# Row sums moved to ScalarE for half of an attention kernel, and mask additions to VectorE for the other half

## The chip, the core and the metric

The kernel runs on one core of one Trainium2 chip. A core has five engines that run their own instruction queues side by side: TensorE (PE, with its weight loads shown apart as PEld), VectorE (DVE), ScalarE (ACT), GpSimd (POOL) and SyncE (SP), which here only starts transfers. The metric is device time in microseconds (us) of one execution; lower is better.

## The reference, cut to what matters

Attention over a window of 64 positions, then a gated feed-forward layer, then a layer of 8 experts of which each token uses one. Only the attention is touched.

```python
batch, n_heads, seq, head_dim = (4, 8, 576, 64)

def _attn_ref(q, k, v):
    scale = 1.0 / np.sqrt(D)
    scores = scale * np.matmul(q, k.transpose(0, 1, 3, 2))
    rel = pos[:, None] - pos[None, :]
    mask = (rel >= 0) & (rel < 64)
    scores = np.where(mask, scores, -1000000000.0)
    scores = scores - np.max(scores, axis=-1, keepdims=True)
    attn = np.exp(scores)
    attn = attn / (np.sum(attn, axis=-1, keepdims=True) + 1e-09)
    return np.matmul(attn, v)

# x = attention output as 2304 x 512
h = (x @ w1) * (x @ w2) @ w3 @ w_out     # first layer, d_ff 1024
# second layer: e = argmax(h @ w_gate); out = gate * relu(h @ w1[e]) @ w2[e]
```

## The kernel before, in words

**Attention.** The 4 batches of 8 heads are handled as 16 pairs of heads, n = 0 to 15, four pairs to a batch (NP is 4). A pair is cut into three groups g, each of three tiles of 128 x 128 scores, so there are 48 groups. A group goes through these steps:

- `score` (L141, L145), PE: a matmul of the identity `idb` with a bf16 mask writes 0 or -1e30 into a PSUM buffer `sps` of 384 columns, and three fp32 matmuls of k and q add the scores to it. Each fp32 matmul shows as two PE instructions.
- `top` (L151, L154), DVE: the maximum of each row, and its negative times 0.125.
- `exps` (L163), ACT: three exponentials of 128 x 128, from `sps` into `pp`.
- `recip` (L168, L170, L172), DVE: the row sums of `pp`, plus 1e-9, and their reciprocal `r`. The small results stand in spare columns of `sps`, so this step ends the use of that buffer.
- `normal` (L177), POOL: `pp` times `r`.
- `turn` (L184), PE: three transposes into a buffer `tps` of the same tag "S", of which there are two in all. `keep` (L189), ACT, copies it out.
- `pv` (L201), PE, and `x_high`, `x_low` (L213, L217) on ACT and DVE make the tokens of the next layer.

**The weights.** The first layer's weights arrive as 64-bit words in 40 chunks. Three DVE instructions for each chunk (L506, L508, L513) turn them into fp32, then ACT (L527) and POOL (L531) split them into a high and a low part. W3 and W_out are multiplied on PE beforehand (L540). The second input matrix can be converted only when all of that product is done, because it takes the slots of W_out.

**The first layer.** For each of nine units of 256 tokens and each of eight steps: two blocks of 12 matmuls (L560), a product and a split on DVE and ACT (L565, L568, L572, L576), and a block of six matmuls (L584). The experts' layer follows.

**Order.** A planner (`Plan`) takes each step with its engine, an assumed duration, a rank and the buffers that it takes and gives, and puts the steps into one order by a simulated list schedule. The order in which instructions are issued on every engine is fixed by that when the program is built, and each engine then takes its instructions strictly in that order. A changed duration of a step can thus move any other step.

Of the kernel before, what the change touches and what calls it, by code (L numbers as in the profile page):

```python
# [9 lines left out]
F32 = mybir.dt.float32  # L10
# [4 lines left out]
AF = mybir.ActivationFunctionType  # L15
ALU = mybir.AluOpType
AX = mybir.AxisListType.X
# [3 lines left out]
B, H, S, D = 4, 8, 576, 64  # L21
NT, DM, DF, NE = B * S, H * D, 1024, 8
NP = H // 2
# [9 lines left out]
class Plan:  # L33
# [5 lines left out]
    def __init__(self, bufs):  # L39
        self.bufs, self.t, self.tag = bufs, [], {}  # L40
# [74 lines left out]
class Attention:  # L115
# [5 lines left out]


    GW = 384

    def __init__(self, tc, pool, ps_s, ps_v, ps_ab, qkv, xunit, ident):
        self.tc, self.nc, self.pool, self.ps_s, self.ps_v = tc, tc.nc, pool, ps_s, ps_v
# [10 lines left out]
    def score(self, n, g):  # L137

        nc, s = self.nc, self.s[n]
        ps = s["S", g] = self.ps_s.tile([128, 512], F32, name="sps", tag="S")  # L140
        nc.tensor.matmul(ps[:, 0:self.GW], lhsT=self.idb, rhs=self.mask[1 if g else 0].rearrange("p a b -> p (a b)"),  # L141
                         start=True, stop=False)
        for i in range(3):
            c = 3 * g + i
            nc.tensor.matmul(ps[:, 128 * i:128 * i + 128], lhsT=s["q"][:, 128 * c:128 * c + 128],  # L145
                             rhs=s["k"][:, 64 * c:64 * c + 128], start=False, stop=i == 2)

    def top(self, n, g):
        nc, s = self.nc, self.s[n]
        ps = s["S", g]  # L150
        nc.vector.tensor_reduce(out=ps[:, 384:387], in_=ps[:, 0:self.GW].rearrange("p (a b) -> p a b", a=3),  # L151
                                axis=AX, op=ALU.max)
        nm = s["nm", g] = self.pool.tile([128, 3], F32, name="nm", tag="nm", bufs=4)
        nc.vector.tensor_scalar(nm, ps[:, 384:387], -0.125, None, op0=ALU.mult)  # L154

    def exps(self, n, g):
        nc, s = self.nc, self.s[n]
        ps = s["S", g]
        nm = s.pop(("nm", g))
        p = s["p", g] = self.pool.tile([128, self.GW], F32, name="pp", tag="pp", bufs=3)  # L160
        for i in range(3):
            o = slice(128 * i, 128 * i + 128)
            nc.scalar.activation(out=p[:, o], in_=ps[:, o], func=AF.Exp, bias=nm[:, i:i + 1], scale=0.125)  # L163

    def recip(self, n, g):
        nc, s = self.nc, self.s[n]
        ps = s.pop(("S", g))
        nc.vector.tensor_reduce(out=ps[:, 392:395], in_=s["p", g].rearrange("p (a b) -> p a b", a=3),  # L168
                                axis=AX, op=ALU.add)
        nc.vector.tensor_scalar(ps[:, 400:403], ps[:, 392:395], 1e-9, None, op0=ALU.add)  # L170
        r = s["r", g] = self.pool.tile([128, 3], F32, name="r", tag="r", bufs=4)
        nc.vector.reciprocal(out=r, in_=ps[:, 400:403])  # L172

# [12 lines left out]
    def keep(self, n, g):  # L186
        s = self.s[n]
        PT = s["PT", g] = self.pool.tile([128, self.GW], F32, name="PT", tag=f"PT{g}", bufs=1)
        self.nc.scalar.activation(out=PT, in_=s.pop(("tp", g))[:, 0:self.GW], func=AF.Copy)  # L189

# [28 lines left out]
    def plan(self, P, n, r, done):  # L219


        def add(name, eng, us, dr, fn, after=(), *a, **kw):
            done[name, n] = P.add(eng, us, r + dr, lambda: fn(n, *a), [done[x] for x in after if x in done], **kw)

        def N(*names):
            return [(x, n) for x in names]

        for i, x in enumerate("qkv"):
            add(x, "DMA", (1.5, 0.8, 1.5)[i], -18 + i, self.load, (), i, take=[(x, (x, n))], lat=2.0)
        for g in range(3):  # L230
            q = -12 + 2 * g
            add(("sc", g), "PE", 0.55, q, self.score, N("q", "k"), g, take=[("S", ("S", n, g))],
                give=[("q", n), ("k", n)] if g == 2 else [])
            add(("top", g), "DVE", 0.72, q, self.top, N(("sc", g)), g)
            add(("exp", g), "ACT", 1.02, q, self.exps, N(("top", g)), g, take=[("pp", ("pp", n, g))])
            add(("rec", g), "DVE", 0.9, q, self.recip, N(("exp", g)), g, give=[("S", n, g)])
            add(("nor", g), "POOL", 0.85, q, self.normal, N(("rec", g)), g)
            add(("tu", g), "PE", 0.36, q, self.turn, N(("nor", g)), g, take=[("S", ("TP", n, g)), (f"PT{g}", ("PT", n, g))],
                give=[("pp", n, g)])
            add(("kp", g), "ACT", 0.5, q, self.keep, N(("tu", g)), g,  # L240
                give=[("TP", n, g)])
        add("pv", "PE", 1.4, -2, self.pv, N("v", *[("kp", g) for g in range(3)]),
            take=[("pv", ("pv", n)), ("ab", ("pvt", n))], give=[("v", n)] + [("PT", n, g) for g in range(3)])
        for tail in (1, 0):
            pc = pieces(n, tail)
            for i, (t0, t1, u, c0) in enumerate(pc):
                us = 0.15 + 0.001 * (t1 - t0)
                give = [("pvt" if tail else "pv", n)] if i == len(pc) - 1 else []
                add(("xh", tail, i), "ACT", us, -1, self.x_high, N("pv") + [("free", u)], tail, i)
                add(("xl", tail, i), "DVE", us, -1, self.x_low, N(("xh", tail, i)), tail, i, give=give)  # L250
                done.setdefault(("unit", u), []).append(done[("xl", tail, i), n])
        done["x", n] = done[("xl", tail, i), n]
# [20 lines left out]
def pieces(n, tail):  # L273

    b = n // NP
    t, end = (512, S) if tail else (0, 512)
    out = []
    while t < end:
        u, c0 = divmod(S * b + t, UNIT)
        w = min(UNIT - c0, end - t)  # L280
        out.append((t, t + w, u, c0))
        t += w
    return out
# [113 lines left out]
def attention_moe_moe_kernel(ctx: ExitStack, tc: tile.TileContext, q0, k0, v, w1, w2, w3, w_out,  # L397
# [316 lines left out]
    def early_rows(part):  # L714

        if part == 0:
            rt.count(256)
            t = idx["early"] = exp_state["p"].tile([128, 2, 2], I32, name="ixe", tag="ixe")
            nc.sync.dma_start(out=t, in_=tab[0:256, :].rearrange("(j p) x -> p j x", p=128))
            g = xg["early"] = moe.tile([128, 4, DM], F32, name="xt1", tag="xt1")  # L720
            nc.vector.memset(g[:, 0:2, :], 0.0)
        else:
            j = part - 1
            top = UNIT * (NU - 1)
            nc.gpsimd.indirect_dma_start(out=xg["early"][:, j, :], out_offset=None, in_=x2d[0:top, :],
                                         in_offset=bass.IndirectOffsetOnAxis(ap=idx["early"][:, j, 0:1], axis=0),
                                         bounds_check=top - 1, oob_is_err=False)
# [375 lines left out]
```

## Time and profile before

| | us |
|---|---|
| median of 3 runs | 787.07 |
| lowest and highest | 786.39, 788.73 |
| the profiled execution | 785.67 |
| its span (first to last instruction) | 784.0 |
| PE busy, share of the span | 734.4, 94% |
| DVE busy | 377.2, 48% |
| ACT busy | 302.0, 39% |

The profile is that of one execution of 785.67 us, of which 1.67 lie outside the span. The shares of the whole span say little here, since the stages differ: in the first 125 us the weights are converted and the first five or so head pairs are done, up to about 440 us the first layer and the rest of the attention run, and the experts fill the rest. The rows below are therefore taken by stage.

### The profile page before, as it was taken

What the parts mean: (1) busy time and instruction counts of PE and PEld (TensorE: products, weight loads), DVE (VectorE), ACT (ScalarE), POOL (GpSimd) and SP (SyncE); (2) the same over time, 40 slices, a digit from 0 to 9 for tenths busy, and PEclk for the clock granted to TensorE, in tenths of its full rate; (3) what the DMA queues carried; (4) which work ended last, traced back from release to release, by engine and by line L of the source; (5) the groups of instructions that cost most, each with busy time, mean ns of one, the idle gap of its engine ahead of it and who ended that gap; (6) DMA issues with size and microseconds to landing.
All of it is one profiled execution on the core that took longest, in us unless ns stands there. A gap on an engine that the chain in (4) does not pass through costs nothing. (4 is left out here: it accounts for less than half of the span.)

```text
span 784.0 us, 13573 instructions
## 1 busy us (share of the span) xinstructions
PE 734.4 (94%) x5227; PEld 658.0 (84%) x5227; DVE 377.2 (48%) x907; ACT 302.0 (39%) x683; POOL 168.1 (21%) x196
## 2 busy tenths in 40 slices
PE   3799989999999999999999999879999999999995
PEld 2577778999999999999999998767888998988874
DVE  6987995543544444444324233813534661661110
ACT  2554443433333243344222123524445563553221
POOL 6554553110111311110020001123112212111010
PEclk9999998999999999999999999999999999999998
DMA  8946762421322222005000001783726772750010
GB/s 326 408 167 217 213 210 84 152 79 31 111 91 87 78 77 77 31 28 189 28 1 28 1 28 48 244 174 109 247 88 233 258 246 90 251 156 28 5 41 14
DMA packets 38934, 97.47 MB, mean 124 GB/s; under 512 B 9748, under 2 KB 9876, under 8 KB 38849
## 3 DMA queue, kind: packets, MB, share of 16 engines
q1 hardware_dynamic: 33072, 83.06, 32.0%
q0 software_dynamic: 4816, 12.77, 5.0%
q8 instruction: 50, 0.82, 0.5%
q10 hardware_dynamic: 960, 0.53, 0.2%
q14 instruction: 36, 0.29, 0.1%
HBM read 86.83 MB, written 10.65 MB: 124 GB/s over the span
## 5 line engine op out<-in xcount | busy, mean ns | idle before, releaser
L560 PE MATMUL ab<-xt,w 128*128 128x256 f32 x1728 | 229.2, 287 | 0.1
L560 PEld LDWEIGHTS ab<-xt,w 128*128 128x128 f32 x1728 | 219.1, 193 | 4.8 <-DVE f L513 0.3
L584 PE MATMUL acc<-w,gt 128*128 128x512 f32 x432 | 114.4, 399 | 3.4 <-ACT gt L572 2.6
L584 PEld LDWEIGHTS acc<-w,gt 128*128 128x128 f32 x432 | 76.1, 189 | 17.4 <-ACT gt L572 3.1
L568 DVE TENSOR_TENSOR a_sb<-ab,a_sb 128x256 f32<-128x256 f32 x72 | 30.5, 423 | 121.9 <-PE ab L560 113.5
L908 PE MATMUL yps<-w,hT 128*128 128x512 f32 x336 | 82.3, 395 | 0.0
L177 POOL TENSOR_TENSOR pp<-pp,r 128x384 f32<-128x384 f32 x48 | 39.6, 828 | 191.7 <-DVE r L172 160.5
L908 PEld LDWEIGHTS yps<-w,hT 128*128 128x128 f32 x336 | 61.3, 188 | 11.6
L572 ACT ACTIVATE gt<-a_sb 128x256 fp32r<-128x256 f32 x72 | 30.0, 416 | 100.3 <-DVE a_sb L568 95.6
L684 DVE TENSOR_TENSOR w<-ck,w 128x1024 fp32r<-128x1024 f32 x48 | 58.1, 1220 | 21.0 <-ACT w L680 14.4
L540 PE MATMUL wps<-w,w3T 128*128 128x512 f32 x192 | 52.7, 417 | 11.7 <-ACT w3T L527 11.6
L680 ACT ACTIVATE w<-ck 128x1024 fp32r<-128x1024 f32 x48 | 50.3, 1057 | 27.0 <-DMA ck<-in_moe_w 24.4
L900 POOL DMA_INDIRECT out<-y,idx x20 | 20.1, 1003 | 178.5 <-ACT y L899 124.1
L163 ACT ACTIVATE pp<-sps,nm 128x128 f32<-128x128 f32 x144 | 42.3, 368 | 39.4 <-DVE nm L154 37.2
L540 PEld LDWEIGHTS wps<-w,w3T 128*128 128x128 f32 x192 | 35.5, 196 | 19.4 <-ACT w3T L527 11.6
L927 PEld LDWEIGHTS hps<-exT,w 128*128 128x128 f32 x384 | 46.4, 192 | 3.5 <-issue 2.2
L927 PE MATMUL hps<-exT,w 128*128 128x256 f32 x384 | 47.4, 284 | 1.9 <-PEq L1049 0.9
L565 ACT ACTIVATE a_sb<-ab 128x256 f32<-128x256 f32 x72 | 27.8, 386 | 55.1 <-PE ab L560 51.9
L389 POOL DMA_INDIRECT tab<-ent,pos x18 | 17.6, 980 | 139.5 <-DVE pos L376 42.2
L422 DVE TENSOR_TENSOR exT<-gps,exT 128x512 fp32r<-128x512 f32 x23 | 15.9, 691 | 58.9 <-ACT exT L421 58.9
L576 DVE TENSOR_TENSOR gt<-a_sb,gt 128x256 fp32r<-128x256 f32 x72 | 31.3, 434 | 25.4 <-ACT gt L572 24.4
L145 PE MATMUL sps<-k,q 128*128 128x128 f32 x288 | 41.4, 282 | 1.0 <-DMA k<-in_k 1.0
(132 smaller groups left out, 1025.6 us busy)
## 6 DMA issues: line engine op xcount, KB each, us to landing
ck<-in_moe_w SPq DMA_DIRECT2D x88, 512.0 KB
q<-in_q SPq DMA_DIRECT2D x16, 576.0 KB
v<-in_v SPq DMA_DIRECT2D x16, 576.0 KB
k<-in_k SPq DMA_DIRECT2D x16, 320.0 KB
w<-in_moe_w_out SPq DMA_DIRECT2D x8, 512.0 KB
w<-in_moe_w SPq DMA_DIRECT2D x8, 512.0 KB
x2d<-x SPq DMA_DIRECT2D x16, 256.0 KB
x2d<-x ACTq DMA_DIRECT2D x2, 256.0 KB
```

Of the source, the lines that this page charges most:

```text
L145: nc.tensor.matmul(ps[:, 128 * i:128 * i + 128], lhsT=s["q"][:, 128 * c:128 * c + 128], rhs=s["k"][:, 64 * c:64 * c + 128], start=False, s ...
L163: nc.scalar.activation(out=p[:, o], in_=ps[:, o], func=AF.Exp, bias=nm[:, i:i + 1], scale=0.125)
L177: nc.gpsimd.tensor_tensor(p, p, s.pop(("r", g)).unsqueeze(2).to_broadcast([128, 3, 128]), op=ALU.mult)
L540: mm(ps, lhsT=t[:, a, 128 * j:128 * j + 128], rhs=wo[b][:, o:o + 512], start=g == 0 and j == 0 and x == 0, stop=g == 1 and j == 3 and x == 2)
L560: mm(ps, lhsT=w[a][:, c:c + 128], rhs=x[:, b, kk, :], start=kk == 0 and i == 0, stop=kk == 3 and i == 2)
L568: V.tensor_tensor(asb[u, m], gps.pop((u, m, 1)), asb[u, m], op=ALU.mult)
L576: V.tensor_tensor(g[:, 1, :], asb.pop((u, m)), g[:, 0, :].bitcast(F32), op=ALU.subtract)
L584: mm(accs[u][t], lhsT=g[:, a, 128 * t:128 * t + 128], rhs=ws["w34"][b][:, 512 * m:512 * m + 512], start=m == 0 and i == 0, stop=m == 7 and ...
L680: nc.scalar.activation(out=eparts()[0], in_=eq[0], func=AF.Copy)
L684: low.tensor_tensor(lo, eq.popleft(), hi.bitcast(F32), op=ALU.subtract)
L908: mm(ps, lhsT=hT[f][:, a, c0:c0 + 128], rhs=w[b][:, 512 * f:512 * f + 512], start=f == 0 and i == 0, stop=f == 7 and i == 2)
L927: mm(ps[:, 0:256], lhsT=w1e[a][:, c:c + 128], rhs=xT[:, b, kk, :], start=kk == 0 and i == 0, stop=kk == 3 and i == 2)
```

## The change

The first two batches (n below `SUMS` = 8, 24 groups) no longer sum `pp` on DVE. The three exponentials of a group write their row sums themselves, through ACT's accumulator output, into a small tile `rs`, and `recip` starts from that. In the last two batches (n from `LATE` = 8 on, 24 groups) the mask matmul is gone from `score`; `top` adds the mask to the scores in PSUM on DVE before the maximum is taken. The planner's assumed durations of these steps are changed to match.

```diff
+    SUMS = 2 * NP
+    LATE = 2 * NP
 ... score
-        nc.tensor.matmul(ps[:, 0:self.GW], lhsT=self.idb, rhs=self.mask[1 if g else 0].rearrange("p a b -> p (a b)"),
-                         start=True, stop=False)
+        late = n >= self.LATE
+        if not late:
+            nc.tensor.matmul(ps[:, 0:self.GW], lhsT=self.idb,
+                             rhs=self.mask[1 if g else 0].rearrange("p a b -> p (a b)"), start=True, stop=False)
...
-                             rhs=s["k"][:, 64 * c:64 * c + 128], start=False, stop=i == 2)
+                             rhs=s["k"][:, 64 * c:64 * c + 128], start=late, stop=late or i == 2)
 ... top
+        if n >= self.LATE:
+            sc = ps[:, 0:self.GW].rearrange("p (a b) -> p a b", a=3)
+            nc.vector.tensor_tensor(sc, sc, self.mask[1 if g else 0], op=ALU.add)
 ... exps
+        rs = s["rs", g] = self.pool.tile([128, 3], F32, name="rs", tag="rs", bufs=4) if n < self.SUMS else None
-            nc.scalar.activation(out=p[:, o], in_=ps[:, o], func=AF.Exp, bias=nm[:, i:i + 1], scale=0.125)
+            nc.scalar.activation(out=p[:, o], in_=ps[:, o], func=AF.Exp, bias=nm[:, i:i + 1], scale=0.125,
+                                 **({} if rs is None else dict(accum_out=rs[:, i:i + 1])))
 ... recip
+        rs = s.pop(("rs", g))
+        if rs is None:
+            rs = ps[:, 392:395]
+            nc.vector.tensor_reduce(out=rs, in_=s["p", g].rearrange("p (a b) -> p a b", a=3), axis=AX, op=ALU.add)
+        nc.vector.tensor_scalar(ps[:, 400:403], rs, 1e-9, None, op0=ALU.add)
 ... plan (the assumed durations, us)
-            add(("top", g), "DVE", 0.72, q, self.top, N(("sc", g)), g)
+            add(("top", g), "DVE", 1.28 if late else 0.72, q, self.top, N(("sc", g)), g)
...
```

The other assumed durations go from 0.55 to 0.38 for the late `score`, from 1.02 to 1.65 for the early `exps` and from 0.9 to 0.4 for the early `recip`.

The first place is on DVE, late in the conversion of the weights, between the maximum of one group and the reciprocal of the same or a near one (`bits` and `f` are the conversions, `a_sb` and `gt` the first layer). Before:

```order
L151 TENSOR_REDUCE sps<-sps 128x3
L506 TENSOR_SCALAR bits<-ck 128x512 x2
L508 SCALAR_TENSOR_TENSOR bits<-ck,bits 128x512 x2
L513 SCALAR_TENSOR_TENSOR f<-ck,bits 128x512 x2
L568 TENSOR_TENSOR a_sb<-ab,a_sb 128x256
L168 TENSOR_REDUCE sps<-pp 128x3
L506 TENSOR_SCALAR bits<-ck 128x512
L170 TENSOR_SCALAR sps<-sps 128x3
L508 SCALAR_TENSOR_TENSOR bits<-ck,bits 128x512
L172 RECIPROCAL r<-sps 128x3
```

The corresponding place now:

```order
L158 TENSOR_REDUCE sps<-sps 128x3
L518 TENSOR_SCALAR bits<-ck 128x512
L161 TENSOR_SCALAR nm<-sps 128x3
L518 TENSOR_SCALAR bits<-ck 128x512
L520 SCALAR_TENSOR_TENSOR bits<-ck,bits 128x512 x2
L525 SCALAR_TENSOR_TENSOR f<-ck,bits 128x512 x2
L580 TENSOR_TENSOR a_sb<-ab,a_sb 128x256
L181 TENSOR_SCALAR sps<-rs 128x3
L158 TENSOR_REDUCE sps<-sps 128x3
L183 RECIPROCAL r<-sps 128x3
```

The sum has left the queue and its successor reads `rs`; six conversions still stand between the maximum and it. On PE, this stretch had two score steps, a block L584, a block L560 and another L584 ahead of the next transposes. Now two score steps, one block of six (L596) and three blocks of twelve (L572) stand there.

The second place is on PE at the first group of the third batch, where a block of the first layer ends. Before:

```order
L560 MATMUL ab<-xt_372,w_1108 128x256
L141 LDWEIGHTS idb
L141 MATMUL sps<-mask_113,idb 128x384
L145 MATMUL sps<-k,q 128x128 x3
L141 LDWEIGHTS idb
L141 MATMUL sps<-mask_114,idb 128x384
L145 MATMUL sps<-k,q 128x128 x3
```

The same place now:

```order
L572 MATMUL ab<-xt_378,w_1107 128x256 x2
L572 MATMUL ab<-xt_378,w_1108 128x256
L149 MATMUL sps<-k,q 128x128 x6
L572 MATMUL ab<-xt_132,w_948 128x256 x2
L572 MATMUL ab<-xt_132,w_949 128x256
```

A weight load and a matmul of 384 columns are gone from each group. Between the second and the third score step stood a block L560, a block L584, another L560 and one step of transposes; now two blocks L572 and one L596 stand there.

The third place is on DVE for the same groups. Before:

```order
L568 TENSOR_TENSOR a_sb<-ab,a_sb 128x256
L151 TENSOR_REDUCE sps<-sps 128x3
L576 TENSOR_TENSOR gt<-a_sb,gt 128x256
L154 TENSOR_SCALAR nm<-sps 128x3
L151 TENSOR_REDUCE sps<-sps 128x3
L154 TENSOR_SCALAR nm<-sps 128x3
L168 TENSOR_REDUCE sps<-pp 128x3
L170 TENSOR_SCALAR sps<-sps 128x3
L172 RECIPROCAL r<-sps 128x3
```

And now:

```order
L580 TENSOR_TENSOR a_sb<-ab,a_sb 128x256
L157 TENSOR_TENSOR sps<-sps,mask_113 128x384
L588 TENSOR_TENSOR gt<-a_sb,gt 128x256
L158 TENSOR_REDUCE sps<-sps 128x3
L157 TENSOR_TENSOR sps<-sps,mask_114 128x384
L161 TENSOR_SCALAR nm<-sps 128x3
L158 TENSOR_REDUCE sps<-sps 128x3
L161 TENSOR_SCALAR nm<-sps 128x3
L180 TENSOR_REDUCE sps<-pp 128x3
L580 TENSOR_TENSOR a_sb<-ab,a_sb 128x256
L181 TENSOR_SCALAR sps<-sps 128x3
L180 TENSOR_REDUCE sps<-pp 128x3
```

Each group has one more instruction, the addition L157, ahead of its maximum, and the second group's addition stands between the first group's maximum and its `nm`.

## Rows read from the trace of the kernel before

**Rows 1.** Stages: length, busy us (instructions) of PE, PEld, DVE, ACT, POOL, PEclk, DMA.

```profile
0.00:40.00 40.00, 22.23 (x129) 16.28 (x130) 32.65 (x76) 16.35 (x38) 24.46 (x53) 0.96 0.95 368
40.00:94.00 54.00, 50.56 (x344) 40.20 (x344) 45.59 (x103) 25.18 (x62) 26.36 (x24) 1.00 0.60 192
94.00:125.00 31.00, 25.64 (x170) 23.46 (x168) 28.12 (x61) 14.71 (x36) 18.76 (x17) 0.89 0.58 198
125.00:440.00 315.00, 314.96 (x2632) 294.78 (x2631) 133.91 (x424) 109.12 (x313) 40.99 (x47) 1.00 0.21 70
```

**Rows 2.** PE's waits from 0 to 125 us: us in total, times, longest.

```profile
PE wps L540 <- ACT w3T L527: 11.6, 1, 11.6
PE tps L184 <- DVE r L172: 7.4, 4, 3.5
PE tps L184 <- POOL pp L177: 2.4, 3, 1.6
...
PE sps L141 <- DVE r L172: 0.9, 1, 0.9
```

**Rows 3.** Timeline of PE, first groups of the third batch: start, duration, line.

```profile
206.67 0.34 PE L141 MATMUL sps<-mask,idb 128*128 128x384 bf16 x1
206.84 0.83 PE L145 MATMUL sps<-k,q 128*128 128x128 f32 x6
207.51 0.33 PE L141 MATMUL sps<-mask,idb 128*128 128x384 bf16 x1
207.67 0.83 PE L145 MATMUL sps<-k,q 128*128 128x128 f32 x6
208.26 1.67 PE L560 MATMUL ab<-xt,w 128*128 128x256 f32 x12
209.77 1.55 PE L584 MATMUL acc<-w,gt 128*128 128x512 f32 x6
211.16 1.59 PE L560 MATMUL ab<-xt,w 128*128 128x256 f32 x12
```

**Rows 4.** Line 141, the whole span: count, ns minimum, median and maximum.

```profile
L141 PEld LDWEIGHTS <-idb x48: 95/96/153, 13.5 to 347.6; 128*128 128x128 bf16 x48
```

**Rows 5.** Timeline of DVE: the reciprocal of the first of these groups.

```profile
210.57 0.18 DVE L172 RECIPROCAL r<-sps 128x3 f32<-128x3 f32 x1
```

**Rows 6.** Groups of DVE's additions and products from PSUM by shape.

```profile
L568 DVE TENSOR_TENSOR a_sb<-ab,a_sb 128x256 f32<-128x256 f32 x72 | 30.5, 423 | 121.9 <-PE ab L560 113.5 <-PE tps L184 3.5 <-issue 2.9
L548 DVE TENSOR_TENSOR w<-wps,w 128x512 fp32r<-128x512 f32 x8 | 5.4, 679 | 2.5 <-ACT w L544 2.5
```

**Rows 7.** Line 168 up to 119.8 us, and up to 94 us.

```profile
L168 DVE TENSOR_REDUCE sps<-pp x16: 544/552/561, 18.8 to 117.2; 128x3 f32<-128x384 f32 x16
...
L168 DVE TENSOR_REDUCE sps<-pp x13: 549/552/561, 18.8 to 87.4; 128x3 f32<-128x384 f32 x13
```

**Rows 8.** Timeline of PE, then of DVE, around PE's longest wait after its start.

```profile
119.30 0.87 PE L184 MATMUL tps<-ident,pp 128*128 128x128 f32 x3 [3.51 <-DVE r L172]
119.83 5.47 PE L560 MATMUL ab<-xt,w 128*128 128x256 f32 x24
...
113.30 1.27 DVE L506 TENSOR_SCALAR bits<-ck 128x512 int32<-128x512 int32 x2
...
117.21 0.54 DVE L168 TENSOR_REDUCE sps<-pp 128x3 f32<-128x384 f32 x1
117.67 0.68 DVE L506 TENSOR_SCALAR bits<-ck 128x512 int32<-128x512 int32 x1
...
118.98 0.17 DVE L172 RECIPROCAL r<-sps 128x3 f32<-128x3 f32 x1
```

**Rows 9.** The stage behind that wait, columns as in rows 1.

```profile
120.00:125.00 5.00, 5.00 (x25) 5.00 (x24) 3.27 (x8) 2.58 (x7) 3.66 (x4) 0.50 0.12 47
```

**Rows 10.** Groups of ACT: the exponentials, and its shortest instruction.

```profile
L163 ACT ACTIVATE pp<-sps,nm 128x128 f32<-128x128 f32 x144 | 42.3, 368 | 39.4 <-DVE nm L154 37.2 <-PE sps L145 1.1 <-DVE r L172 0.7
L374 ACT ACTIVATE ez<-zs 128x2 f32<-128x2 f32 x3 | 0.6, 198 | 1.1 <-DVE zs L372 1.1
```

More of the change, by code (lines that the diff above doesn't have):

```diff
@@ L167, in recip @@
         ps = s.pop(("S", g))
-        nc.vector.tensor_reduce(out=ps[:, 392:395], in_=s["p", g].rearrange("p (a b) -> p a b", a=3),
-                                axis=AX, op=ALU.add)
-        nc.vector.tensor_scalar(ps[:, 400:403], ps[:, 392:395], 1e-9, None, op0=ALU.add)
+        rs = s.pop(("rs", g))
[3 more added lines that the diff above has]
+        nc.vector.tensor_scalar(ps[:, 400:403], rs, 1e-9, None, op0=ALU.add)
         r = s["r", g] = self.pool.tile([128, 3], F32, name="r", tag="r", bufs=4)
@@ L231, in plan @@
             q = -12 + 2 * g
-            add(("sc", g), "PE", 0.55, q, self.score, N("q", "k"), g, take=[("S", ("S", n, g))],
+            late = n >= self.LATE
+            add(("sc", g), "PE", 0.38 if late else 0.55, q, self.score, N("q", "k"), g, take=[("S", ("S", n, g))],
                 give=[("q", n), ("k", n)] if g == 2 else [])
-            add(("top", g), "DVE", 0.72, q, self.top, N(("sc", g)), g)
-            add(("exp", g), "ACT", 1.02, q, self.exps, N(("top", g)), g, take=[("pp", ("pp", n, g))])
-            add(("rec", g), "DVE", 0.9, q, self.recip, N(("exp", g)), g, give=[("S", n, g)])
+            add(("top", g), "DVE", 1.28 if late else 0.72, q, self.top, N(("sc", g)), g)
+            add(("exp", g), "ACT", 1.65 if n < self.SUMS else 1.02, q, self.exps, N(("top", g)), g, take=[("pp", ("pp", n, g))])
+            add(("rec", g), "DVE", 0.4 if n < self.SUMS else 0.9, q, self.recip, N(("exp", g)), g, give=[("S", n, g)])
             add(("nor", g), "POOL", 0.85, q, self.normal, N(("rec", g)), g)
```

## The prediction

> **What bounds the kernel now.** I read the stages first, then PE's waits, then the timeline at the places where the change acts. The stages [rows 1] show two regimes. From 125 to 440 us PE is busy 314.96 of 315 us at the full clock: whatever PE no longer has to do there comes off the time, as long as it never has to wait. DVE (133.91) and ACT (109.12) are busy under half of it. Before 125 us it is the other way round: DVE is busy 32.65 of 40, 45.59 of 54 and 28.12 of 31 us, while PE idles for 125 - 22.23 - 50.56 - 25.64 = 26.6 us. Of these 11.6 are the start, before the first weights are there [rows 2]. Most of the rest stands behind the end of the softmax: 7.4 us for the reciprocal and 2.4 for POOL's product behind it before transposes, and 0.9 for the reciprocal before a score, 10.7 in all [rows 2]. That is where DVE's queue holds up PE.
>
> So the two halves of the change act on two different bounds, and I cost them apart.
>
> **The mask matmuls of the last two batches.** 24 of the 48 go [rows 4], all in the stage in which PE is full. The row says 0.33 us for each, but matmuls overlap: from the start of the mask matmul to the start of the next it is 206.84 - 206.67 = 0.17 and 207.67 - 207.51 = 0.16 us [rows 3]. 24 x 0.165 = **4.0 us**. The bounds are 0, if PE then waits for something else, and 24 x 0.33 = 7.9, if the whole row were paid. I take 4.0, since it is PE's own pace at just this place.
>
> In exchange DVE adds the mask to 128 x 384 scores. No row shows that addition. Its neighbours are 0.42 us for 256 columns and 0.68 for 512 from PSUM [rows 6]; half-way is 0.55. 24 x 0.55 = 13.2 us more on an engine that has 181 us free in the stage: hidden as work. What could show is the delay. The maximum queues behind the addition, the exponentials behind the maximum, and the score buffer comes free only at the reciprocal. In the trace the first group's scores start at 206.67 and its reciprocal ends at 210.75 [rows 3, 5], 4.1 us. Now 0.17 is gone and 0.55 added for itself, and the second group's addition stands in front of its `nm`, another 0.55 at most: 5.0 us. By the new order PE has two score steps (2 x 0.67), two blocks of twelve (2 x 1.5) and one of six (1.4) before the third group needs the buffer: 5.7 us by their paces [rows 3]. The cover is 0.7 us here. I cost the delay at nothing; if the cover is gone, each group pays up to its addition.
>
> **The row sums of the first two batches.** 24 sums leave DVE, 16 of them before 119.8 us [rows 7]; the other 8 are in the stage where PE is full and are worth nothing. A sum occupies DVE's queue for 117.67 - 117.21 = 0.46 us until the next starts [rows 8], so DVE gets 16 x 0.46 = 7.4 us back. ACT pays: the trace has no accumulator output, so I bound it. Below, nothing; above, one more instruction like the exponential itself for each, 0.368 us; the nearest small one takes 0.198 us [rows 10], which I take. 48 x 0.2 = 9.6 us on an ACT that is busy 56.2 of 125 us [rows 1] is hidden as work. In the chain of one group it is 3 x 0.2 = 0.6 later on ACT against 0.46 earlier on DVE: as a delay the two cancel. The gain is then only what a shorter DVE queue gives PE.
>
> Up to 94 us, 13 of the 16 sums [rows 7] can give 6.0 us at most, and nothing if only the delay counts; below nothing too, if ACT's extra is 0.368 (3 x 0.368 - 0.46 = 0.64 for a group, 8.4 for 13 groups, if all were exposed). Between 40 and 94 us PE idles only 3.4 us [rows 1], and before 40 the transfers run at 0.95 of what they can, so they hold up the conversions as well. I take 2.5.
>
> From 94 to 125 us one wait stands out: PE idles 3.51 us before the transposes at 119.30, and the next 24 matmuls take 5.47 us [rows 8] where 12 take 1.51 (208.26 to 209.77) [rows 3]. The granted clock there is 0.50, that is 1.2 instead of 2.4 GHz [rows 9]. The wait costs 3.5 and the slow clock behind it 5.47 - 3.0 = 2.4. Its cause is in DVE's queue: six conversions from 113.30 on stand in front of the sum of a group whose exponentials were long done. The new order leaves the six conversions there, but puts three blocks of twelve and one of six on PE where one and two stood: 2 x 1.5 - 1.4 = 1.6 us more cover, and 0.46 from the sum. About 1.5 of the 3.5 stay. I count 2.0 for the wait and half of the slow clock, 1.2: 3.2 us. The bounds are 0 and 5.9.
>
> **The sum.** 4.0 + 2.5 + 3.2 = 9.7 us. The profiled execution took 785.67, so 776.0. The median of the three runs is 1.4 above that execution; I add 1.0 and forecast **777.0**, 1.3% under the median. A change of less than 0.3% (2.4 us) can't be told from none with this kernel.
>
> **The rivals.**
>
> - *The front gives nothing.* The sum and ACT's extra cancel in the chain, DVE stands idle for ACT instead of summing, and PE waits as before. For it: the chain adds up to +0.14 a group, and the six conversions are still in front of the reciprocal. Against it: DVE is the busiest engine until 125 us. Only the mask counts: 785.67 - 4.0 + 1.0 = 782.7.
> - *The weight loads pace PE, not the matmuls.* PEld is busy 294.78 of the 315 us [rows 1]. If the loads are the limit, a mask group gives back its one load of 0.096 us [rows 4] and not 0.165: 24 x 0.096 = 2.3, and the time is 1.7 higher, 778.7. Against it: the six matmuls of a score step follow each other in 0.11 us each [rows 3], so loads overlap each other. The Trainium skill ("Trainium Kernel Development and Optimization", Performance Expectations) holds matmul busy time to be a bad measure and the busy share of the weight loads to be a good one, which speaks for this rival; the trace has both above 93% in this stage and doesn't decide.
> - *PE waits in the full stage (slower).* The additions lengthen the hold on one of two score buffers. It decides where PE's work between a score step and the next user of its buffer falls under the chain; at the place worked out above 0.7 us are left, and first-layer products on DVE in between can use them up. The price if every addition is exposed is 24 x 0.55 = 13.2 us, and with the slow clock that follows a long wait more. With the front at nothing: 785.67 - 4.0 + 13.2 + 1.0 = 795.9; with half of the groups exposed and the front at half of its 5.7, 786.4, no change. Against it: PE has no wait in 315 us before, and the new order keeps more blocks there.
> - *The front gives all.* 6.0 + 5.9 + 4.0 = 15.9: 770.8. For it: each of these waits is behind DVE's queue. Against it: conversions still stand in front of the reciprocals.
>
> **How the numbers follow.** The forecast with both halves 0.48, the front at nothing 0.17, weight loads 0.10, the front at all 0.10, PE waiting in the full stage 0.15 (half of it within 0.3%, half slower). The unknown price of the accumulator adds a little to the slower side, since at 0.368 and more it could make the front a loss. Faster by over 0.3% (under 784.7): 0.48 + 0.17 + 0.10 + 0.10 = 0.85, less 0.06 for that, 0.79. Of the 0.21 left, 0.10 is within 0.3% and 0.11 slower. The range goes from 770.0, the front at all, to 785.5, where the front gives nothing and a part of the additions shows. About 0.16 lies above it and 0.04 below.
>
> **What would show it.** In the full stage of the new profile: no L141 counterpart after about 200 us, PE still busy without a wait, and the score steps starting 0.67 us apart. A wait of PE for the maximum, the exponentials or the reciprocal after 125 us would show the third rival. In the front: the stage in which PE is full should begin some 5 us sooner, PE's waits for the reciprocal and POOL should fall from 10.7 to about 6 us, and the stretch at clock 0.50 should shrink. On ACT, the exponentials of the first two batches show the price of the accumulator, by longer rows or by rows of their own; over 0.4 us each I have costed the front wrongly. If the first layer's last block does not end about 10 us sooner than the 440 us of now, the forecast is wrong.

## The result and the profile after

The changed kernel took 779.1 us (median of 4 runs, 778.2 to 779.81), the kernel before 786.73 beside it (785.6 to 788.73). The ratio is 0.9912 with an interval of 0.9893 to 0.993: 0.88% faster, some 6.9 us. The forecast was 777.0; the sum behind it had 9.7 us off the profiled 785.67, and the two profiled executions differ by 785.67 - 779.81 = 5.9. Lines of the new kernel are numbered higher: mask matmul L145, scores L149, the new addition L157, maximum L158, exponentials L171, the remaining sums L180, reciprocal L183, POOL's product L188, transposes L195, the product of W3 and W_out L552, the first layer's blocks L572 and L596.

First the stages of the kernel after, with the columns of [rows 1]:

```profile
0.00:40.00 40.00, 22.27 (x123) 16.22 (x123) 29.38 (x68) 16.98 (x55) 23.57 (x52) 0.96 0.95 361
40.00:94.00 54.00, 50.13 (x339) 40.53 (x340) 43.12 (x96) 27.97 (x84) 28.45 (x26) 0.98 0.63 216
94.00:125.00 31.00, 28.09 (x222) 25.19 (x222) 28.52 (x61) 16.07 (x49) 17.30 (x16) 0.97 0.49 166
125.00:440.00 315.00, 314.78 (x2609) 295.27 (x2608) 138.79 (x441) 109.58 (x336) 42.29 (x47) 1.00 0.21 70
```

Subtract PE's busy time from each length. Up to 40 us PE idles 17.73 us (17.77 before), from 40 to 94 us 3.87 (3.44), from 94 to 125 us 2.91 (5.36). So the sums bought PE nothing before 94 us, although DVE was busy 3.27 and 2.47 us less there, and 2.4 us after it. In the full stage PE is still busy but for 0.2 us.

PE's waits from 0 to 125 us (total, times, longest), to be held against [rows 2]:

```profile
PE wps L552 <- ACT w3T L539: 11.5, 1, 11.5
PE tps L195 <- POOL pp L188: 7.0, 5, 3.5
PE tps L195 <- DVE r L183: 1.6, 1, 1.6
PE sps L145 <- DVE r L183: 1.3, 1, 1.3
```

The wait for the reciprocal before transposes fell from 7.4 to 1.6 us, but that for POOL's product rose from 2.4 to 7.0. With the wait for the reciprocal before scores (0.9, now 1.3), 10.7 us became 9.9.

These two waits are for different things. POOL's product is the data that the transposes read. The reciprocal belongs to another group: it ends the use of a score buffer, and the transposes need a buffer of the same tag "S". The trace of before shows it at the longest wait:

```profile
110.61 0.83 POOL L177 TENSOR_TENSOR pp<-pp,r 128x384 f32<-128x384 f32 x1 [0.45 <-DVE r L172]
...
119.54 0.83 POOL L177 TENSOR_TENSOR pp<-pp,r 128x384 f32<-128x384 f32 x1
```

The transposes at 119.30 [rows 8] start before the product at 119.54 that uses the reciprocal of 118.98, so they read an earlier product; the last one was done at 111.44. They waited for a buffer alone. The prediction took the two waits for two steps of one chain.

PE's timeline at three places (start, duration; the idle time before it in brackets):

```profile
27.23 0.86 PE L195 MATMUL tps<-ident,pp 128*128 128x128 f32 x3 [3.53 <-POOL pp L188]
...
91.00 0.55 PE L195 MATMUL tps<-ident,pp 128*128 128x128 f32 x3 [1.87 <-POOL pp L188]
91.30 4.59 PE L552 MATMUL wps<-w,w3T 128*128 128x512 f32 x12
...
112.00 0.49 PE L195 MATMUL tps<-ident,pp 128*128 128x128 f32 x3
...
116.53 0.49 PE L195 MATMUL tps<-ident,pp 128*128 128x128 f32 x3
117.96 1.69 PE L572 MATMUL ab<-xt,w 128*128 128x256 f32 x12 [0.94 <-DVE f L525]
```

The last three lines answer to [rows 8]: the same group's transposes, now at 116.53, no longer wait, and the block behind them runs at full pace. Those at 112.00 are now the first behind the pair of score steps and need the buffer that the pair's first reciprocal gives back:

```profile
110.20 0.17 DVE L183 RECIPROCAL r<-sps 128x3 f32<-128x3 f32 x1
```

It ends 1.6 us ahead of them. But 3.53 us now stand at 27 us, and the twelve matmuls at 91.30 took 4.59 us. Both of these waits are for POOL's product, and POOL's own queue has a part in them. Its rows at the second, before and then after:

```profile
89.16 0.17 DVE L172 RECIPROCAL r<-sps 128x3 f32<-128x3 f32 x1
89.40 0.83 POOL L177 TENSOR_TENSOR pp<-pp,r 128x384 f32<-128x384 f32 x1
...
88.65 0.17 DVE L183 RECIPROCAL r<-sps 128x3 f32<-128x3 f32 x1
88.88 1.28 POOL L543 TENSOR_TENSOR w<-f,w 128x512 fp32r<-128x512 f32 x1 [1.01 <-ACT w L539]
90.12 0.82 POOL L188 TENSOR_TENSOR pp<-pp,r 128x384 f32<-128x384 f32 x1
```

In these two executions DVE delivered the reciprocal 0.5 us sooner, but a weight split (L543) now stands between it and the product on POOL. The product starts 1.30 us after the reciprocal's end instead of 0.07, and the transposes start 0.7 us later (91.00 instead of 90.28). At 27 us it is the same: the reciprocal ends at 25.40, the product starts at 26.35 behind a split, where before it followed its reciprocal by 0.14 us.

The granted clock behind 91.30, by stages of 2 us:

```profile
92.00:94.00 2.00, 2.00 (x7) 1.57 (x6) 0.00 (x0) 0.07 (x1) 0.00 (x0) 0.54 0.44 168
94.00:96.00 2.00, 2.00 (x7) 1.32 (x7) 0.01 (x1) 0.07 (x1) 0.00 (x0) 0.60 0.00 0
```

So a stretch of mostly 1.2 GHz, as behind the long wait in [rows 9], now lies here. In a second profiled execution of the same kernel (the last experiment below) the same twelve took 2.98 us at full clock. DVE does nothing in these rows, and its timeline says why:

```profile
89.32 0.68 DVE L525 SCALAR_TENSOR_TENSOR f<-ck,bits 128x512 int32<-128x512 int32 x1
95.98 0.17 DVE L323 MEMSET onb<- 128x128 bf16 x1 [5.99 <-PE wps L552]
```

Its next instruction in order, a small memset, waits for PE's product W3 x W_out, and the conversions that could fill the gap wait for the same product (their slots are W_out's). DVE ran ahead of PE and then stood for 5.99 us (0.8 before).

Last, the two new kinds of instruction (ns minimum, median, maximum), and the first accumulated group:

```profile
L171 ACT ACTIVATION_READ_ACCUMULATOR pp<-sps,nm x72: 188/199/218, 17.6 to 167.5; 128x1 f32 x72
...
L157 DVE TENSOR_TENSOR sps<-sps,mask x24: 556/567/567, 188.1 to 341.4; 128x384 f32<-128x384 f32 x24
```

```profile
17.30 0.37 ACT L171 ACTIVATE pp<-sps,nm 128x128 f32<-128x128 f32 x1 [0.19 <-DVE nm L161]
17.57 0.19 ACT L171 ACTIVATION_READ_ACCUMULATOR pp<-sps,nm 128x1 f32 x1
17.66 0.36 ACT L171 ACTIVATE pp<-sps,nm 128x128 f32<-128x128 f32 x1
```

These answer to [rows 6, 10]. The accumulator is an instruction of its own of 0.199 us. It starts 0.27 us into its exponential, which lasts 0.37, and the next exponential starts 0.36 us after the first. Over the whole trace the median step is 0.34 us with the accumulator and 0.25 without, so it costs ACT's queue 0.09 us and not 0.199.

### The profile page after: what moved, and what is told of

Same layout as the page of the kernel before. It is cut to its first block, busy times and chain, and to the rows that moved or that the text cites. A ratio compares the mean times of both kernels' runs of the same rounds, so it can differ in the third digit from the quotient of the medians.

```text
span 778.0 us, 13569 instructions
## 1 busy us (share of the span) xinstructions
PE 729.4 (94%) x5203; PEld 654.2 (84%) x5203; DVE 375.9 (48%) x907; ACT 306.7 (39%) x755; POOL 169.0 (22%) x196
## 5 line engine op out<-in xcount | busy, mean ns | idle before, releaser
L572 PE MATMUL ab<-xt,w 128*128 128x256 f32 x1728 | 228.1, 285 | 1.6 <-DVE f L525 0.9
L572 PEld LDWEIGHTS ab<-xt,w 128*128 128x128 f32 x1728 | 216.6, 191 | 6.5 <-DVE f L525 1.7
L596 PE MATMUL acc<-w,gt 128*128 128x512 f32 x432 | 114.3, 400 | 1.7 <-ACT gt L584 1.7
L596 PEld LDWEIGHTS acc<-w,gt 128*128 128x128 f32 x432 | 76.1, 189 | 15.0 <-ACT gt L584 1.9
L188 POOL TENSOR_TENSOR pp<-pp,r 128x384 f32<-128x384 f32 x48 | 40.9, 856 | 195.2 <-DVE sps L181 84.2
L580 DVE TENSOR_TENSOR a_sb<-ab,a_sb 128x256 f32<-128x256 f32 x72 | 30.4, 422 | 109.0 <-PE ab L572 99.3
L584 ACT ACTIVATE gt<-a_sb 128x256 fp32r<-128x256 f32 x72 | 30.0, 416 | 95.7 <-DVE a_sb L580 91.1
L552 PE MATMUL wps<-w,w3T 128*128 128x512 f32 x192 | 54.0, 428 | 11.6 <-ACT w3T L539 11.5
L577 ACT ACTIVATE a_sb<-ab 128x256 f32<-128x256 f32 x72 | 27.6, 384 | 80.4 <-PE ab L572 77.1
L171 ACT ACTIVATE pp<-sps,nm 128x128 f32<-128x128 f32 x144 | 46.8, 370 | 25.9 <-DVE nm L161 16.4
L552 PEld LDWEIGHTS wps<-w,w3T 128*128 128x128 f32 x192 | 37.1, 202 | 19.5 <-ACT w3T L539 11.5
L149 PE MATMUL sps<-k,q 128*128 128x128 f32 x288 | 41.2, 285 | 1.0 <-DMA k<-in_k 0.8
```

What stands on the lines that cost most here:

```text
L188: nc.gpsimd.tensor_tensor(p, p, s.pop(("r", g)).unsqueeze(2).to_broadcast([128, 3, 128]), op=ALU.mult)
L552: mm(ps, lhsT=t[:, a, 128 * j:128 * j + 128], rhs=wo[b][:, o:o + 512], start=g == 0 and j == 0 and x == 0, stop=g == 1 and j == 3 and x == 2)
L572: mm(ps, lhsT=w[a][:, c:c + 128], rhs=x[:, b, kk, :], start=kk == 0 and i == 0, stop=kk == 3 and i == 2)
L580: V.tensor_tensor(asb[u, m], gps.pop((u, m, 1)), asb[u, m], op=ALU.mult)
L596: mm(accs[u][t], lhsT=g[:, a, 128 * t:128 * t + 128], rhs=ws["w34"][b][:, 512 * m:512 * m + 512], start=m == 0 and i == 0, stop=m == 7 and ...
```

## The late batches, at the place where the cover was worked out

PE and then DVE of the kernel after, around the first group of the third batch:

```profile
187.25 1.50 PE L149 MATMUL sps<-k,q 128*128 128x128 f32 x12
188.50 3.12 PE L572 MATMUL ab<-xt,w 128*128 128x256 f32 x24
193.12 0.91 PE L149 MATMUL sps<-k,q 128*128 128x128 f32 x6
...
188.12 0.57 DVE L157 TENSOR_TENSOR sps<-sps,mask 128x384 f32<-128x384 f32 x1 [0.17 <-PE sps L149]
188.59 0.41 DVE L588 TENSOR_TENSOR gt<-a_sb,gt 128x256 fp32r<-128x256 f32 x1
188.92 0.56 DVE L158 TENSOR_REDUCE sps<-sps 128x3 f32<-128x384 f32 x1
...
191.95 0.41 DVE L580 TENSOR_TENSOR a_sb<-ab,a_sb 128x256 f32<-128x256 f32 x1
...
192.35 0.55 DVE L180 TENSOR_REDUCE sps<-pp 128x3 f32<-128x384 f32 x1
192.81 0.17 DVE L183 RECIPROCAL r<-sps 128x3 f32<-128x3 f32 x1
```

ACT stands between the two parts of DVE's timeline:

```profile
190.29 0.39 ACT L577 ACTIVATE a_sb<-ab 128x256 f32<-128x256 f32 x1 [1.89 <-PE ab L572]
190.57 1.66 ACT L171 ACTIVATE pp<-sps,nm 128x128 f32<-128x128 f32 x6
```

Two things are read here. Two score steps took 188.50 - 187.25 = 1.25 us until the next block, and 208.26 - 206.67 = 1.59 with masks [rows 3]: 0.17 us for each mask matmul, PE's pace, and not the 0.096 of its weight load. It is so in all 24 late steps: their mean was 0.787 us and is 0.617, and PE waits in front of none. And the first group holds its buffer from 187.25 to 192.98, 5.7 us, not 5.0; the score step that takes it next starts at 193.12. The cover was 0.14 us, not 0.7.

Of the 1.65 us that the hold is longer than in [rows 3, 5], 0.76 lie up to the end of `nm`, where the two additions are; the forecast had 0.93 there. Another 0.44 stand in front of the exponentials, which now wait behind a first-layer instruction on ACT (L577), and 0.45 between the sum and the end of the reciprocal, where DVE does a first-layer sum (L580) and the second group's row sum (L180).

## Experiments

All were timed beside the kernel before on the same chip; the ratio is to that, with its interval. "Old durations" are the planner's assumed ones of before.

One thing has to be known for these runs. The planner's order is binding on PE alone: the kernel holds `tc.manual_schedule(engines={E.PE})`, and the instructions of the other engines are put into an order of their own when the program is built. It is not so that the planner fixes the order on every engine, as was assumed ahead of the prediction. The run of the sums alone with the old durations has the same planner numbers as the kernel before. Up to 125 us of the trace of before, all 638 PE instructions come in the same order in both, but those of DVE, ACT and POOL do not: before, POOL's third product (25.52 us) comes ahead of a weight split (26.31), and in that run it comes behind it (26.42 and 25.19). So "old order" and "new order" below are PE's, and the orders of DVE, ACT and POOL follow from the operations as well. No run here separates the two.

**Only the masks.** `SUMS` to 0; the late groups and their durations as in the change.

```diff
-    SUMS = 2 * NP
+    SUMS = 0
```

> Only the second part: the last two batches add their masks on VectorE, the row sums stay on VectorE everywhere; the front is ordered as before. Theory (PE's own pace): 24 x 0.165 = 4.0 us less, ratio 0.995, and no wait of PE between 125 and 440 us. Rival (weight loads pace PE): 24 x 0.096 = 2.3 us less, ratio 0.997. Rival (the additions are exposed): no gain or a loss, and PE waits for the maximum, exponentials or reciprocal after 200 us.

Measured: 781.65 against 785.06 us, 0.9957 (0.994 to 0.9974). That is 3.4 us, interval 2.0 to 4.7. PE has no wait from 125 to 440 us, and in the front it waits 7.1 us for the reciprocal before transposes, as before. The forecast's 4.0 lies inside the interval, and so does 2.3 by weight loads; the 24 score steps above decide between the two.

**Only the sums.** `LATE` past the last pair.

```diff
-    LATE = 2 * NP
+    LATE = 4 * NP
```

> Only the first part: the first two batches' row sums by the accumulator, masks by matmul everywhere; the front is ordered as in the changed kernel. Theory: the front's gain alone, 2.7 us by the two profiles (the first layer ends 6.7 us sooner, less 4.0 for the masks), ratio 0.9965; the product W3 W_out still ends near 95 us and VectorE idles some 6 us ahead of the memset behind it. Rival: all of the changed kernel's gain comes from the masks, ratio 1.000.

Measured: 781.21 against 785.06, 0.9957 (0.994 to 0.9975): 3.4 us as well (forecast: 2.7), so the rival that the masks make all of the gain is out. Most of it lies in the stage from 94 to 125 us, with PE busy for 28.04 us at full clock. The product of W3 and W_out ends at 93.6 us here and DVE stands for 4.5 us behind it, not until near 95 and for 6:

```profile
94.00:125.00 31.00, 28.04 (x229) 25.65 (x228) 30.17 (x65) 17.40 (x54) 19.06 (x17) 1.00 0.54 185
```

The two halves add up: 0.43% and 0.43% against 0.88% together.

**All operations of the change, old durations.** Only the planner's numbers are put back.

```diff
-            add(("sc", g), "PE", 0.38 if late else 0.55, q, ...
+            add(("sc", g), "PE", 0.55, q, ...
-            add(("top", g), "DVE", 1.28 if late else 0.72, q, ...
-            add(("exp", g), "ACT", 1.65 if n < self.SUMS else 1.02, q, ...
-            add(("rec", g), "DVE", 0.4 if n < self.SUMS else 0.9, q, ...
+            add(("top", g), "DVE", 0.72, q, ...
+            add(("exp", g), "ACT", 1.02, q, ...
+            add(("rec", g), "DVE", 0.9, q, ...
```

> All operations of the changed kernel, but the planner keeps the durations of before, so the order of the front is that of before, with the sums gone from VectorE's queue. Theory (the new order, which puts more matmuls in front of the transposes near 119 us, makes the front's gain): the 3.5 us wait there shrinks only by the sum's 0.46 us, the front gains under 1 us, and the time is 0.5 to 3 us above the changed kernel, 780 to 782. Rival (the shorter queue makes it, the order doesn't matter): the same time as the changed kernel, 779. Second rival: in the late batches the planner doesn't know of the additions, so PE waits after 200 us and the time is above 782.

Measured: 789.57 against 785.06, 1.0068 (1.0051 to 1.0086). The same operations, with PE in the old order, are slower than before. Its full stage, and PE's waits in it:

```profile
125.00:440.00 315.00, 307.64 (x2539) 286.64 (x2537) 140.35 (x437) 108.01 (x328) 41.59 (x46) 1.00 0.21 69
```

```profile
PE tps L195 <- POOL pp L188: 5.2, 7, 1.1
PE sps L149 <- DVE sps L181: 1.5, 1, 1.5
PE sps L149 <- DVE r L183: 0.6, 1, 0.6
```

PE idles 7.4 us where it idled none. That is the third rival of the prediction, at a price of 7.3 us in waits and not 13.2, and mostly not before scores: POOL's product comes later, and the transposes stand too early in PE's queue.

**No accumulator.** The changed kernel, its order on PE included, with the early row sums left out and a constant in their place (some of DVE's and ACT's instructions change places by it).

```diff
-        rs = ... pool.tile([128, 3], F32, name="rs", tag="rs", bufs=4)
+        rs = ... self.one
-                 accum_out=rs[:, i:i + 1]
```

> The changed kernel in its own order, but the row sums of the first two batches are left out: no accumulator output, and a constant in their place. It takes away ACT's 72 accumulator reads (0.199 us each) and nothing else. Theory A (the front's gain is held down by the wait behind the product W3 W_out, the reads are hidden): within 1 us of the changed kernel, 778 to 779.5. Theory B (the reads lie in the chain that PE waits for, 0.6 us for a group): PE's waits for POOL's product before transposes, 7.0 us in the changed kernel, fall to under 4, and the time falls by 2 to 5 us, 774 to 777.

Measured: 777.08, 0.9901 (0.9886 to 0.9916) against 0.9912 for the change. The two differ by 0.0011, some 0.9 us, which can't be told from none: the 72 reads, 14.3 us by their rows, are hidden as far as can be seen. PE's waits for POOL before transposes are still 6.3 us: ACT's extra work isn't what makes most of them.

**The order alone.** Operations of before, assumed durations of after; PE's order is that of the changed kernel, with the late mask matmuls kept.

```diff
-            add(("sc", g), "PE", 0.55, q, ...
+            add(("sc", g), "PE", 0.38 if n >= 2 * NP else 0.55, q, ...
-            add(("top", g), "DVE", 0.72, q, ...
-            add(("exp", g), "ACT", 1.02, q, ...
-            add(("rec", g), "DVE", 0.9, q, ...
+            add(("top", g), "DVE", 1.28 if n >= 2 * NP else 0.72, q, ...
+            add(("exp", g), "ACT", 1.65 if n < 2 * NP else 1.02, q, ...
+            add(("rec", g), "DVE", 0.4 if n < 2 * NP else 0.9, q, ...
```

> The operations of before, in the order that the changed kernel's assumed durations give: row sums on VectorE and masks by matmul everywhere. With the order of before and the changed operations the time was 0.7% above before, so order and operations were taken apart only from one side. Theory (gain needs both: the order gives the transposes near 119 us their cover, the sums off VectorE's queue let the rest keep up): a part of the front's gain, 0 to 2 us, ratio 0.9975 to 1.000. Rival (the order alone makes the whole front gain): ratio 0.9957, as with the sums alone. Rival (the new order without the new operations is a loss): over 1.002, with PE waiting for the reciprocal or POOL's product before 125 us for over 13 us in all.

Measured: 788.55 against 784.95, 1.0047 (1.0031 to 1.0063). PE's waits up to 125 us, apart from the start:

```profile
PE tps L184 <- POOL pp L177: 7.8, 5, 3.0
PE sps L141 <- DVE r L172: 3.4, 3, 2.0
PE tps L184 <- POOL w L531: 2.5, 1, 2.5
PE tps L184 <- DVE r L172: 1.0, 1, 1.0
```

14.7 us where these waits were 10.7 before; 12.2 of them are for the reciprocal and POOL's product, a little under the "over 13" of the rival. Other waits of before are gone, so that all of PE's idle time up to 125 us went from 26.6 to 27.8 only, and 0.8 were added in the full stage; the first layer's last block starts 2.7 us later. The time is 3.6 us longer: the new order without the new operations is a loss.

**Sums alone in the old order.** The four old durations as above, and:

```diff
-    LATE = 2 * NP
+    LATE = 4 * NP
```

> The first part alone (row sums of the first two batches by the accumulator, all masks by matmul), but in the order of before: the planner keeps the old durations. So far the sums in the new order gave 0.43% and the new order without the sums cost 0.47%. Theory (the front's gain needs the sums and the order together): ratio 0.998 to 1.002, with the wait of PE near 119 us still over 2 us. Rival (the sums alone give it, the order only has to fit the masks): ratio 0.996, as with the sums in the new order.

Measured: 784.86 against 784.87, 1.0001 (0.9985 to 1.0017). PE at the place of [rows 8]:

```profile
118.90 0.52 PE L195 MATMUL tps<-ident,pp 128*128 128x128 f32 x3 [1.60 <-DVE r L183]
119.18 1.67 PE L572 MATMUL ab<-xt,w 128*128 128x256 f32 x12
```

The wait shrank from 3.51 to 1.60 and the slow clock behind it is gone, which I had not expected without the new order. But PE now waits 2.9 us in one piece for the first layer's `gt` from DVE, up to 104.07 us (0.8 in the run with the masks alone in this order, next), and the slow stretch has moved there:

```profile
104.00:106.00 2.00, 1.93 (x6) 1.61 (x7) 2.00 (x6) 0.71 (x3) 1.82 (x2) 0.62 0.58 203
106.00:108.00 2.00, 2.00 (x12) 2.00 (x11) 0.48 (x1) 0.53 (x1) 1.54 (x2) 0.53 0.70 160
```

PE's idle time up to 125 us is 27.0 us (26.6 before). The waits changed places, and the time did not move.

**Masks alone in the old order.** The four old durations as above, and:

```diff
-    SUMS = 2 * NP
+    SUMS = 0
```

> The second part alone (masks of the last two batches on VectorE, sums on VectorE everywhere), in the order of before: the planner doesn't know of the additions. In its own order this part gave 0.43%. Theory (the additions lengthen the chain from the scores to the product, and only the new order covers it): PE waits 7 us between 200 and 350 us, for POOL's product and the reciprocal, so 4.0 less and 7 more, ratio 1.003 to 1.005. Rival (the loss seen with both parts in the old order came from the front): ratio 0.996 as in its own order, and no waits after 125 us.

Measured: 791.17 against 784.87, 1.0085 (1.0061 to 1.0108).

PE is busy for 307.65 of the 315 us of the full stage and waits 7.3, by the same three releasers as in the run with all operations and old durations. Against the 4.0 that the masks give back that is +3.3, and the first layer's last block starts at 494.7 instead of 491.4 us: just that. The time is 6.3 us longer, though. Some 1.2 are in the experts' stage of the profiled execution, whose span is 4.5 longer. The other 1.8 are between the executions: the profiled one lies 1.0 under the median of this run, and that of before, from another chip, 0.8 over the median beside it.

**Conversions let go earlier.** In the changed kernel the slots of W_out are waited for only by the splits of the second input matrix, not by the first of its three conversion steps.

```diff
-  t0 = P.add("DVE", 0.6, r, lambda: convert(i, 0), [L] + old, ...)
+  t0 = P.add("DVE", 0.6, r, lambda: convert(i, 0), [L], ...)
-  hi = P.add("ACT", 0.63, r + 2, lambda: high(i), after, ...)
+  hi = P.add("ACT", 0.63, r + 2, lambda: high(i), after + old, ...)
```

> The changed kernel, but the conversions of the second input matrix no longer wait in the plan for the end of W3 W_out (only ACT's write into the freed slot does). Theory (VectorE, ahead of PE since the sums are gone, runs out of permitted work behind the product: it idles 6.0 us at the memset near 96 us): the idle time falls to 3 us or less, PE's waits after 95 us (2.8 us for conversions, reciprocal and first-layer products) fall to under 1.5, and the time falls by 1 to 3 us, 776 to 778. Rival (PE alone sets the front by then): VectorE's idle time moves elsewhere and the time stays at 779.

Measured: 777.65 against 784.95, 0.9904 (0.988 to 0.9928): not to be told from the change's 0.9912. DVE's wait at the memset went from 6.0 to 1.0 us, so the gap was closed, but PE's waits up to 125 us are now these, the last of them new:

```profile
PE tps L195 <- POOL pp L188: 6.9, 5, 3.4
PE ab L572 <- DVE f L525: 2.4, 1, 2.4
PE acc L596 <- DVE gt L588: 1.7, 1, 1.7
```

All of PE's idle time up to 125 us is 25.7 us, not less than the change's 24.5. So closing DVE's gap moved PE's waits and gained nothing that can be told from none.

**The masks moved from the pair n = 6 on.** 6 instead of 8.

```diff
-    LATE = 2 * NP
+    LATE = 6
```

> The changed kernel with the mask on VectorE from pair 6 on instead of 8: 6 more groups, all behind 125 us. Theory (each mask matmul in the full stage is worth PE's pace, 0.165 us): 6 x 0.165 = 1.0 us less than the changed kernel, 778. Rival (two PSUM score buffers are held longer, so a busier stage makes PE wait): 0 to 3 us more, with waits of PE for POOL's product or the reciprocal between 125 and 190 us.

Measured: 776.91 against 784.95, 0.9891 (0.987 to 0.9911), with 0.9 us of PE waits in the full stage. It is the lowest ratio of all, but its interval overlaps the change's: six groups more would be worth 6 x 0.17 = 1.0 us, which is under what can be told here.

**Both of the last two edits.** The two lines of the conversions as above, and:

```diff
-    LATE = 2 * NP
+    LATE = 6
```

> Both of the two runs before together: early conversions and the mask on VectorE from pair 6 on. Theory: their gains add, 2 to 4 us under the changed kernel, 775 to 777. Rival: the front's gain is taken back in the stage behind it, since the order from 95 to 190 us moves as well: at or above 779.

Measured: 778.27 against 784.95, 0.9922 (0.9896 to 0.9948), 1.6 us of PE waits in the full stage. The expected 2 to 4 us under the changed kernel did not come. The intervals of the three runs overlap, so that whether one edit takes back what the other gives is not shown.

**The changed kernel again**, unedited, on the chip of the two runs of one half in the old order.

> The changed kernel itself, unaltered, beside the two others and before on one chip, so that its ratio and its waits have a second reading. All theories expect 0.991 again; the reading also shows how far the end of W3 W_out (95.4 us) and VectorE's idle time at the memset (6.0 us) vary between executions of one program.

Measured: 776.42 against 784.87, 0.9906 (0.9877 to 0.9935). Its profiled execution has a span of 774.0 us, 4.0 under the first, and these rows from PE:

```profile
90.03 0.55 PE L195 MATMUL tps<-ident,pp 128*128 128x128 f32 x3 [1.66 <-POOL pp L188]
90.34 2.98 PE L552 MATMUL wps<-w,w3T 128*128 128x512 f32 x12
```

DVE waited 4.5 us at the memset here and the product ended at about 93 us as in the kernel before, and not past 95. So the 1.6 us of slow clock around 94 us belong to the first profile's execution; DVE's idle time behind the product does not. PE's idle time up to 94 us is 21.4 us, again no less than before.

## Why the prediction came out as it did

The runs that cross operations and PE's order, as ratios to before:

| operations | PE's old order | PE's new order |
|---|---|---|
| of before | 1 | 1.0047 |
| sums moved | 1.0001 | 0.9957 |
| masks moved | 1.0085 | 0.9957 |
| both | 1.0068 | 0.9912 |

Each cell of the new order was planned with the durations that fit its own operations, except the first, which has those of both. Neither the operations nor PE's order gain by themselves.

- **Mask matmuls, 4.0 us: right.** 0.17 us each in the timeline of all 24 steps, 24 x 0.17 = 4.1, and 3.4 us in time (2.0 to 4.7). Weight loads do not pace PE at these steps, although they are busy 94% of the stage.
- **The addition, 0.55 us, hidden: right, but with less to spare than said.** It takes 0.567 us. Hidden it is only in the new order, and at the worked-out place by 0.14 us and not 0.7: I let only the two additions into the chain, but in the new order a first-layer instruction on ACT and a first-layer sum and a second row sum on DVE stand in it, too. The two on DVE were in the order shown ahead of the prediction. The third rival at 0.15 was a real danger; its price is 7.3 us of waits, and the planner's durations decide it.
- **The accumulator, 0.2 us: right in size** (0.199), and hidden. It overlaps its exponential, so a group's chain grows by about 0.28 us (two steps longer by 0.09 and 0.09 behind the last exponential) and not by 0.6. The chain thus got shorter, since the sum's 0.46 left it; the two do not cancel.
- **The front up to 94 us, 2.5 us: failed.** PE idles 21.6 us there instead of 21.2, and 21.4 in the second execution. The step that failed is "the gain is then only what a shorter DVE queue gives PE", sized at 2.5 by 13 sums. That holds only where DVE is the last that PE waits for. Transposes need two things, a buffer from another group's reciprocal and their own group's product from POOL. The shorter queue shortened the first wait, and the second then ended last. At 27 and 91 us weight splits in POOL's queue held the product back by 0.95 and 1.3 us. In the total the first rival was right here, though not by its mechanism: its chain of ACT and DVE got shorter. What the waits for POOL cost was not tried; the run that closed DVE's idle time gained nothing that can be told.
- **From 94 to 125 us, 3.2 us: the wait went, for more reasons than forecast.** All of the 3.51 us is gone and not merely 2.0, and so is all of the slow clock's 2.4. From the first group's `nm` to its reciprocal DVE needed 6.2 us and needs 3.9. The forecast took 0.46 of this off, for the sum; the two conversions between the sum and the reciprocal are gone from there as well, as the order ahead of the prediction already shows. That the term still came out near is in part luck: PE has other waits of 2.8 us in the stage (1.8 before), so that its idle time fell by 2.4.
- **The sum.** In the profiled executions PE idles 26.6 - 24.5 = 2.1 us less in the front, and the slow stretches behind 90 us cost 1.6 instead of 2.4, 0.8 less (before 40 us both have one, mean clock 0.96 in both). With 4.0 for the masks that makes 6.9; the first layer's last block starts at 484.7 instead of 491.4, 6.7 sooner, where I had about 10. Of these, 0.7 are given back in the experts' stage, where PE's wait for the routing rose from 2.2 to 3.5 us. The front term was mis-sized: 5.7 forecast, some 3 measured (3.4 by the run with the sums alone). That is why 779.1 is between the forecast and the 782.7 of a front that gives nothing.
- **The signs.** PE has no mask matmul from 187 us on, no wait of over 0.6 us in the full stage, and score steps 0.62 us apart, as forecast. The waits for the reciprocal and POOL fell to 9.9 us and not to about 6. The last sign named 440 us, but the first layer's last block starts at 491.4 us in the trace of before. It came 6.7 us sooner where about 10 were asked: by this sign, too, the front was forecast too high.

What stays open: what a product ahead of the weight splits on POOL would give, how much of each order's effect lies on PE and how much on the engines that the planner does not bind, whether the two late edits add, and whether the masks from n = 6 on beat the change.

## What to carry to other kernels

Where a fixed order is planned from assumed durations, an operation and its duration in the plan are one change: here the same operations run from 0.9912 to 1.0068 of the time by those numbers alone. See also which engines the plan binds: here PE alone, and the others changed places with the operations. Relief of an engine pays only as far as the one that waits has that engine as its last releaser. Before the gain is counted, see for each wait whether it is for data or for a buffer, and what would release it next (here POOL's product, behind POOL's own weight splits). The cost of a matmul that overlaps others is the step between starts in the timeline, not its row's duration.

## What the runs showed of the hardware

An accumulated exponential of 128 x 128 brings a second ACT row, ACTIVATION_READ_ACCUMULATOR, of 0.188 to 0.218 us, which starts about 0.1 us before the exponential's own row ends; the step from one exponential to the next went from 0.25 to 0.34 us. An addition of a bf16 mask to 128 x 384 scores in PSUM took 0.567 us on DVE. And TensorE's slow stretch is not a property of the program alone: the same twelve matmuls of the changed kernel ran at a granted clock of 0.54 to 0.60 (mostly 1.2 GHz) in one execution, after PE had idled for 1.87 us, and at full speed in another, after 1.66 us.
